# Hash attention and a gated feed-forward block in one kernel: the first unit's gates in groups of three, its value means in the output bank, its first value cast and loads placed elsewhere, and idle products in four slots

## The chip, the cores and the metric

The kernel runs on one core of a Trainium2 chip. A core has five engines that run side by side and wait for one another by semaphores: PE (TensorE, matmuls and transposes, which write to PSUM), DVE (VectorE), ACT (ScalarE), POOL (GpSimd) and SP (SyncE, which here only issues DMAs). ACT and POOL issue DMAs too. Each engine works through its own instructions in the order in which the program gives them. The metric is the device time of one execution in microseconds (us).

## The reference

Two stages, in float32 in and out. The kernel computes matmul operands in 16 bits where the code says so.

```python
q_bits = (np.einsum('bhsd,dk->bhsk', q, proj) > 0)      # 6 bits per token and head
k_bits = (np.einsum('bhsd,dk->bhsk', k, proj) > 0)
mask = q_bucket[:, :, :, None] == k_bucket[:, :, None, :]
scores = np.where(mask, scale * np.matmul(q, k.transpose(0, 1, 3, 2)), -1e9)
attn = softmax(scores)                                   # sum + 1e-9 below the line
x = (attn @ v) as rows of 512                            # 4 batches x 768 tokens = 3072 rows
xn = x / np.sqrt(np.mean(x * x, axis=-1, keepdims=True) + 1e-06) * rms_g
g = xn @ w_gate                                          # 512 -> 1536
out = (g / (1 + np.exp(-g)) * (xn @ w_val)) @ w_out      # 1536 -> 512
```

There are 4 batches, 8 heads of 64, 768 tokens, a model width of 512 and a feed-forward width of 1536.

## The kernel before, in words

**Units and slots.** The 3072 rows are worked through in half batches of 384 tokens, called w = 0 to 7, three blocks of 128 tokens each. The first half batch is split: unit 0 is its first block, unit 1 its other two; units 2 to 8 are whole half batches (`UNITS`, L32). A unit runs over the 8 heads, and each head takes as many slots as the unit has blocks, so unit 0 has slots 0 to 7, unit 1 slots 8 to 23, and later units 24 slots each. A slot is one bank pair of scores (`scores`, L345 to L355, tile s_ps, two buffers) and one exponential over 128x768 on ACT (`probs`, L361, tile psb). The hash mask is part of the score product: 12 rows of signed bits stand under the 64 rows of q and k (tile QK, 76 rows), so that one matmul gives scores with unequal buckets pushed far down.

**The first heads.** For batch 0, `turn_head` transposes k and q of a head on PE (t_ps, L167), copies k to SBUF on DVE and q on ACT (L175), casts k to 16 bits on POOL (`cast_half`, L179) and the first part of q on ACT. `hash_head` (L243) makes the projections on PE (d_ps, L219), DVE turns them into signed bits (`signs`, L226), and the bits go into the QK rows: one or two pieces by a DVE copy (L258), one by ACT, for every second head one more by ACT, the rest by DMA (`late_bits`).

**Products with values.** `av` multiplies the exponentials by the values (o_ps, L375; the output bank has one buffer for a pair of heads). Values are cast to 16 bits on POOL (`v_prep`, L300, tile vl). A column of ones beside the values gives the sum of each row. `v_mean` (L311) sums the values of all tokens of a batch with a matmul by ones into a bank of its own (m_ps, from the three banks of the pool `gps`) and scales them into cvb; `attn_out` adds cvb to the output bank (otmp, L391), takes the reciprocal and multiplies (x, L399: on POOL, for the last pair of heads on DVE). In batch 0 the scaling is done by ACT (L319).

**Norm and feed-forward.** `norm` takes the mean square, the power -1/2 (POOL, L441) and scales rows (xn, L445); `turn_x` transposes them (x_ps, L453) and multiplies by the gain (xnT, L454). `gate` and `value` take one of 12 blocks of the feed-forward width at a time: four matmuls for the gate (g_ps, L470), tanh on ACT (t, L472), four matmuls for the value (v_ps, L481), and two DVE instructions (a, L483; ht, L484). `project` multiplies by the output weights (y_ps, L495), ACT copies the result (ysb, L502) and SP sends it out (L504).

**What sets the order.** The order is written by hand. `plan` holds steps for every slot; `at(s, f, ..., rank=3)` puts a step there, and `steps(s)` sorts a slot's steps by rank and, within a rank, by the order in which they were put down (L583 to L589). In the main loop (L713) a slot s issues the scores of slot s+1 and the exponential of slot s, and then its steps; from slot 24 on, steps of rank below 3 come first, then the exponential of slot s+1, and then the others. `work` (L612) lists for each pair of heads of batches 1 to 3 in which slots its three loads are issued and in which its four transposes are made. `ffn` (L681) spreads the 12 gates and 12 values of a unit over a stretch of slots; a step whose slot is already taken by one of them gets rank 4. Loads go through SP in program order, into ten buffers; SP waits for a buffer's last reader. Weights go through POOL's queue (L543, L549).

Of the kernel before, what the change touches and what calls it, by code (L numbers as in the profile page):

```python
# [16 lines left out]
S = 768  # L17
# [24 lines left out]
def kernel(  # L42
# [188 lines left out]
    def bit_rows(b, h, t):  # L231
        return QK[b, h // 2][D:KROWS, h % 2, t * HALF : (t + 1) * HALF]
# [4 lines left out]
    def bits_tile(i):  # L237
# [3 lines left out]
        return held[-1][:, (i % 2) * HALF : (i % 2 + 1) * HALF]  # L241

    def hash_head(h, n=HALF, k0=None, k1=None):  # L243
        kt, qt = t0(0, h, "k"), t0(0, h, "q")
        ps = hash_bank(
            [(pk[:, 0:32], kt), (pq[:, 0:32], qt), (pk[:, 12:44], kt), (pq[:, 12:44], qt)]
        )
        bt = bits_tile(h)
        signs(bt, ps)
        nc.scalar.copy(bit_rows(0, h, 1)[:, 0:n], bt[32:44, 0:n])  # L250
        for eng, t in ((k0, 0), (k1, 2)):
            src = bt[32 * t : 32 * t + 12]
            if eng is nc.scalar:
                nc.scalar.copy(bit_rows(0, h, t), src)
            elif eng is nc.sync:
                nc.sync.dma_start(out=bit_rows(0, h, t), in_=src)
            else:
                nc.vector.tensor_copy(bit_rows(0, h, t), src)  # L258
        late[h] = bt
# [50 lines left out]
    def v_mean(b, hp, n, parts=(None,)):  # L310
        hs = slice(2 * hp, 2 * hp + n)  # L311
        ps = bank("m_ps", [128, n, 65])
        for i, jt in enumerate(parts):
# [3 lines left out]
            )  # L317
        if b == 0:
            nc.scalar.mul(cvb[b % 2][:, hs, 0:65], ps, C0 / S)  # L319
        else:  # L320
            nc.vector.tensor_scalar_mul(cvb[b % 2][:, hs, 0:65], ps, C0 / S)

# [42 lines left out]
    def av(u, h, i0, i1):  # L365
# [6 lines left out]
        for i in range(i0, i1):  # L372
# [89 lines left out]

    def gate(u, ft):
        w, cs, n = columns(u)
        fs = slice(ft * 128, (ft + 1) * 128)
# [9 lines left out]
    def value(u, ft, gt):  # L475
        g, t = gt
        w, cs, n = columns(u)
        fs = slice(ft * 128, (ft + 1) * 128)
        vv = bank("v_ps", [128, HALF])[:, 0:n]
        for kt in range(4):  # L480
            nc.tensor.matmul(vv, wv[:, kt, fs], xnT[w][:, kt, cs], start=(kt == 0), stop=(kt == 3))  # L481
        a = spool.tile([128, HALF], FP32, name="a")[:, 0:n]
        nc.vector.scalar_tensor_tensor(out=a, in0=t, scalar=1.0, in1=g, op0=ALU.add, op1=ALU.mult)  # L483
        nc.vector.scalar_tensor_tensor(  # L484
            out=ht[w][:, ft, cs], in0=a, scalar=0.5, in1=vv, op0=ALU.mult, op1=ALU.mult
        )
# [3 lines left out]
    def project(w, c, f0, f1):  # L490
# [8 lines left out]
        if f1 == NF:  # L499
# [112 lines left out]
    work = {  # L612
# [50 lines left out]
    for u, (w, c0, n) in enumerate(UNITS):  # L663
        for h in range(H):
            last = BASE[u] + n * h + n - 1
            if n == 1:
                at(last + 1, av, u, h, 0, 6)
                end = last + 1
# [4 lines left out]
            if h % 2:  # L673
                at(end, o_step, u, h // 2)
                if h < 7:
                    if u > 0:
                        at(end + 2 * n, s_step, u, h // 2)
                elif u < 8:
                    at(end, norm, u)

    def ffn(u, s0, ns):  # L681

        seen = set()
        for ft in range(NF):
            for f, s in ((g_step, s0 + (ns * ft) // NF),
                         (v_step, s0 + (2 * ns * ft + ns) // (2 * NF))):
                at(s, f, u, ft, rank=4 if s in seen else 2)
# [100 lines left out]
```

## Time and profile before

| | |
|---|---|
| median of 3 runs | 349.87 us (349.87 to 351.09) |
| profiled execution, its own time | 349.89 us |
| its span, first to last instruction | 348.1 us |
| mean granted TensorE clock | 0.984 |
| PE busy | 334.9 us (96%) |
| DVE busy | 238.2 us (68%) |
| ACT busy | 216.7 us (62%) |
| POOL busy | 138.6 us (40%) |

How to read the profile: the page gives busy times of each engine, the span in 40 equal slices (8.7 us each; a digit is tenths busy; PEclk is the clock that TensorE was granted, in tenths of full speed), and the chain of work that ended last, followed back from the last instruction. A row of a group or of the timeline has the source line, the engine, the operation and the tiles as out<-in, with partitions x elements. A timeline row begins with the start and the duration in us; in [..] stands the idle time of the engine before it and what ended it. The chain's rows have start, duration and what ran. Rows of stretches give, for each stretch, its length and the busy time and number of instructions of PE, PEld (the weight loads, which overlap PE), DVE, ACT and POOL, the granted clock, the share of the DMA engines and GB/s.

### The profile page before, as it was taken

The page shows a single profiled execution, that of the slowest core. Times are in us where ns is not written, and L with a number is a line of the kernel's source. Part 1 is how long each engine was busy: PE and PEld are TensorE (multiplying, and loading weights), DVE is VectorE, ACT ScalarE, POOL GpSimd, SP SyncE. Part 2 cuts the span into 40 slices and gives each one's busy share as a digit, 9 for nine tenths or more (in the row PEclk, how much of TensorE's full clock was granted, in tenths as well). Part 3 has the DMA queues.
Part 4 walks back from the last instruction along what each step waited for, and adds up shares of the span by engine and source line. Part 5 has one row for each costly group of instructions (what it writes and reads, how often), then busy time and mean ns, then how long its engine had stood idle before and what let it go on. Part 6 is the DMA issues. An engine that isn't in the chain of part 4 may idle for free.

```text
span 348.1 us, 8206 instructions
## 1 busy us (share of the span) xinstructions
PE 334.9 (96%) x3172; PEld 212.5 (61%) x3172; DVE 238.2 (68%) x541; ACT 216.7 (62%) x361; POOL 138.6 (40%) x220
## 2 busy tenths in 40 slices
PE   8897998999999999999999999999999999999995
PEld 5456886666666655665566656665566656665553
DVE  3784566688678955897678866897467555675860
ACT  2587687677567755766567756775576766742321
POOL 5476544777214751286126551385111111111000
PEclk9997799999999999999999999999999999999999
DMA  7999944273399005930376008600200010001002
GB/s 216 322 237 190 246 169 89 41 130 80 61 174 149 3 6 145 185 48 5 81 179 119 3 16 200 122 2 6 73 32 1 2 60 33 2 2 74 16 3 90
DMA packets 80199, 31.42 MB, mean 90 GB/s; under 512 B 65240, under 2 KB 77216, under 8 KB 80160
## 3 DMA queue, kind: packets, MB, share of 16 engines
q1 hardware_dynamic: 76176, 26.11, 32.1%
q0 software_dynamic: 3680, 4.72, 7.9%
q8 instruction: 25, 0.41, 0.5%
q14 instruction: 14, 0.11, 0.1%
q10 hardware_dynamic: 304, 0.07, 0.1%
HBM read 28.32 MB, written 6.29 MB: 99 GB/s over the span
## 4 chain that ended last, share of the span: by engine, by line
PE 82%; DVE 11%; issue 3%; ACT 2%; POOL 2%; DVEq 0%; POOLq 0%; ACTq 0%
PE g_ps L470 17%; PE v_ps L481 17%; PE s_ps L351 16%; PE y_ps L495 15%; PE o_ps L375 9%; PE d_ps L219 3%; DVE bits L226 2%; PE x_ps L453 2%; DVE otmp L391 1%; DVE QK L258 1%; DVE xn L445 1%; DVE kT L175 1%; PE y_ps L745 1%; PE m_ps L315 1%; DVE kT L203 1%
## 5 line engine op out<-in xcount | busy, mean ns | idle before, releaser
L361 ACT ACTIVATE psb<-s_ps 128x768 f16<-128x768 f32 x192 | 151.8, 809 | 26.6 <-PE s_ps L351 26.3
L351 PE MATMUL s_ps<-QK 76*128 76x384 f16 (+2 forms) x448 | 96.6, 310 | 0.7 <-ACT psb L361 0.2
L472 ACT ACTIVATE t<-g_ps 128x384 f32<-128x384 f32 (+2 forms) x108 | 49.2, 456 | 55.7 <-PE g_ps L470 54.7
L470 PE MATMUL g_ps<-xnT,wg 128*128 128x384 f16 (+2 forms) x432 | 80.6, 309 | 1.2 <-DVE xnT L454 0.8
L481 PE MATMUL v_ps<-xnT,wv 128*128 128x384 f16 (+2 forms) x432 | 80.6, 309 | 0.7 <-DVE a L483 0.6
L495 PE MATMUL y_ps<-wo,ht 128*128 128x512 f16 x276 | 69.1, 378 | 0.3
L483 DVE SCALAR_TENSOR_TENSOR a<-t,g_ps 128x384 f32<-128x384 f32 (+2 forms) x108 | 53.9, 499 | 21.5 <-ACT t L472 19.8
L375 PEld LDWEIGHTS <-psb 128*128 128x128 f16 x1152 | 52.9, 99 | 19.3 <-issue 5.3
L484 DVE SCALAR_TENSOR_TENSOR ht<-a,v_ps 128x384 f16<-128x384 f32 (+2 forms) x108 | 55.1, 510 | 13.1 <-PE v_ps L481 3.3
L375 PE MATMUL o_ps<-vl,psb 128*128 128x65 f16 x1152 | 58.7, 195 | 2.1 <-DVE otmp L391 1.8
L399 POOL TENSOR_TENSOR x<-otmp,rcp 128x384 f32<-128x384 f32 (+2 forms) x27 | 20.4, 756 | 99.7 <-DVE rcp L396 99.5
L351 PEld LDWEIGHTS <-QK 76*128 76x128 f16 x448 | 40.0, 101 | 25.2 <-issue 1.7
L470 PEld LDWEIGHTS <-wg 128*128 128x128 f16 x432 | 39.2, 97 | 24.1 <-issue 2.9
L481 PEld LDWEIGHTS <-wv 128*128 128x128 f16 x432 | 39.3, 98 | 22.7 <-issue 1.2
L495 PEld LDWEIGHTS <-ht 128*128 128x128 f16 x276 | 24.1, 97 | 20.9 <-issue 0.5
L502 ACT COPY ysb<-y_ps 128x512 f32<-128x512 f32 x23 | 13.5, 586 | 29.4 <-PE y_ps L495 29.1
L391 DVE TENSOR_TENSOR otmp<-o_ps,cvb 128x390 f32<-128x390 f32 (+2 forms) x36 | 18.5, 513 | 17.1 <-PE o_ps L375 14.7
L454 DVE TENSOR_TENSOR xnT<-x_ps,gcol 128x512 f16<-128x512 f16 x24 | 16.6, 691 | 12.7 <-PE x_ps L453 12.6
L211 POOL CAST QK<-kT 64x768 f16<-64x768 f32 x20 | 16.4, 820 | 17.9 <-DVE kT L203 11.6
L226 DVE TENSOR_SCALAR bits<-d_ps,thr,scl 128x384 f16<-128x384 f32 x20 | 13.2, 677 | 12.9 <-PE d_ps L219 12.7
L211 POOL CAST QK<-qT 64x768 f16<-64x768 f32 x20 | 16.4, 820 | 11.9 <-DVE qT L203 11.0
L413 POOL TENSOR_TENSOR sq<-x 128x384 f32<-128x384 f32 (+1 forms) x24 | 19.2, 800 | 1.9
(74 smaller groups left out, 281.6 us busy)
## 6 DMA issues: line engine op xcount, KB each, us to landing
vL<-in_v_dram SPq DMA_DIRECT2D x16, 384.0 KB
out_dram<-ysb SPq DMA_DIRECT2D x23, 256.0 KB
kL<-in_k_dram SPq DMA_DIRECT2D x40, 96.0 KB
qL<-in_q_dram SPq DMA_DIRECT2D x40, 96.0 KB
kL<-in_k_dram SPq DMA_DIRECT2D x5, 384.0 KB
qL<-in_q_dram SPq DMA_DIRECT2D x5, 384.0 KB
wg<-in_moe_w_gate_dram POOLq DMA_DIRECT2D x2, 768.0 KB, 10.6
wv<-in_moe_w_val_dram POOLq DMA_DIRECT2D x2, 768.0 KB, 8.9
```

What stands on the lines that cost most here:

```text
L211: nc.gpsimd.tensor_copy(QK[b, hp][0:64, hh, o : o + S], T0[b, hp, which][64 * hh : 64 * hh + 64, :])
L351: nc.tensor.matmul(ps[:, bk, col : col + ni], k_cols(b, h, jt), q_cols(w, h, 128 * c0 + i0, ni), start=True, stop=True,)
L361: nc.scalar.activation(psb[u, h][:, p], sps.pop(g)[:, :, 0:HALF], AF.Exp, scale=ESCALE,)
L375: nc.tensor.matmul(o[:, c, hh, 0:65], psb[u, h][:, p, bk, col : col + 128], vls[b % 2][:, h, v_chunk(b, h, jt), 0:65], start=(hh == 0 and ...
L391: nc.vector.tensor_add(tmp[:, 0:n, :, 0:65], o[:, 0:n, :, 0:65], cvb[b % 2][:, 2 * hp : 2 * hp + 2, 0:65].unsqueeze(1).to_broadcast([128, ...
L399: eng.tensor_mul(xd.rearrange("p c (h d) -> p c h d", h=2), tmp[:, 0:n, :, 0:64], r[:, 0:n].to_broadcast([128, n, 2, 64]),)
L470: nc.tensor.matmul(g, wg[:, kt, fs], xnT[w][:, kt, cs], start=(kt == 0), stop=(kt == 3))
L472: nc.scalar.activation(t, g, AF.Tanh, scale=0.5)
L481: nc.tensor.matmul(vv, wv[:, kt, fs], xnT[w][:, kt, cs], start=(kt == 0), stop=(kt == 3))
L483: nc.vector.scalar_tensor_tensor(out=a, in0=t, scalar=1.0, in1=g, op0=ALU.add, op1=ALU.mult)
L484: nc.vector.scalar_tensor_tensor(out=ht[w][:, ft, cs], in0=a, scalar=0.5, in1=vv, op0=ALU.mult, op1=ALU.mult)
L495: nc.tensor.matmul(y, ht[w][:, ft, c * 128 : (c + 1) * 128], wo[:, ft, :], start=(ft == 0), stop=(ft == NF - 1),)
```

## The change

- **Bits.** The DVE copies of bits into QK in `hash_head` become `move`: one `scalar_tensor_tensor` that adds zero to the source and takes the maximum with the same source, which leaves the value as it is. There are 13 of them.
- **Value means of batch 0.** `mean0` makes the sums in the output bank of the same pair of heads, in the part that unit 0 leaves unused (its block 1), behind the first of the pair's two products; ACT scales them as before. `v_mean` is used for the later batches alone and stays on DVE there.
- **Value casts.** The first goes ahead of the casts of heads 2 and 3 on POOL; the others are put into slots 1, 3 and 4 at rank 1.
- **Idle products.** `idle(g, n)` makes n products of ones by ones, 128 columns wide, into columns of the next slot's score bank that nothing reads: 6 in slot 4 and 12 in each of slots 5, 6 and 7, 42 in all, as the last step of the slot.
- **Groups.** In unit 0 a step of `gate` or `value` takes three blocks of the feed-forward width at once: 12 matmuls into one bank, one tanh and two DVE instructions over 128x384. The other units keep single blocks.
- **Order.** In unit 0 `av` and `attn_out` get rank 1; in later units `attn_out`, its sum of squares and `norm` get rank 5. The loads of batch 1's first two pairs of heads go three or four slots earlier, their transposes up to five slots earlier, and unit 1's two `turn_x` steps one slot later.
- **First output.** The DMA of the first output block is issued by ACT instead of SP.

```diff
+    def move(dst, src):
+        nc.vector.scalar_tensor_tensor(
+            out=dst, in0=src, scalar=0.0, in1=src, op0=ALU.add, op1=ALU.max
+        )
...
-                nc.vector.tensor_copy(bit_rows(0, h, t), src)
+                move(bit_rows(0, h, t), src)
...
-        if b == 0:
-            nc.scalar.mul(cvb[b % 2][:, hs, 0:65], ps, C0 / S)
-        else:
-            nc.vector.tensor_scalar_mul(cvb[b % 2][:, hs, 0:65], ps, C0 / S)
+        nc.vector.tensor_scalar_mul(cvb[b % 2][:, hs, 0:65], ps, C0 / S)
...
+    def mean0(hp):
+        for c in range(6):
+            nc.tensor.matmul(
+                ot[0, hp][:, 1, :, 0:65], ones16, vls[0][:, 2 * hp : 2 * hp + 2, c, 0:65],
+                start=False, stop=(c == 5), skip_group_check=True,
+            )
+        nc.scalar.mul(cvb[0][:, 2 * hp : 2 * hp + 2, 0:65], ot[0, hp][:, 1, :, 0:65], C0 / S)
+
+    def idle(g, n):
+        for _ in range(n):
+            nc.tensor.matmul(
+                sps[g][:, 1, HALF:], ones16, ones16, start=True, stop=True,
+                skip_group_check=True,
+            )
...
+    GROUP = [3] + 8 * [1]
...
-        g = bank("g_ps", [128, HALF])[:, 0:n]
-        for kt in range(4):
-            nc.tensor.matmul(g, wg[:, kt, fs], xnT[w][:, kt, cs], start=(kt == 0), stop=(kt == 3))
-        t = spool.tile([128, HALF], FP32, name="t")[:, 0:n]
+        g = bank("g_ps")[:, 0 : k * n]
+        for j in range(k):
+            fs = slice((f0 + j) * 128, (f0 + j + 1) * 128)
+            for kt in range(4):
+                nc.tensor.matmul(
+                    g[:, j * n : (j + 1) * n], wg[:, kt, fs], xnT[w][:, kt, cs],
+                    start=(kt == 0), stop=(kt == 3),
+                )
+        t = spool.tile([128, HALF], FP32, name="t")[:, 0 : k * n]
...
-            nc.sync.dma_start(out=rows[:, out_chunk(w, c), :], in_=ysb)
+            eng = nc.scalar if (w, c) == (0, 0) else nc.sync
+            eng.dma_start(out=rows[:, out_chunk(w, c), :], in_=ysb)
...
+    v_prep(0, 0)
     turn_head(2, 128)
...
-    for hp, s in enumerate((0, 1, 3, 4)):
-        at(s, v_prep, 0, hp)
+    for hp, s in ((1, 1), (2, 3), (3, 4)):
+        at(s, v_prep, 0, hp, rank=1)
...
-        at(2 * hp + 2 if hp < 3 else 7, v_mean, 0, hp, 2, range(6))
+        at(2 * hp + 1, mean0, hp, rank=2)
...
-        (1, 0): ((21, 22, 23), (28, 29, 30, 31)), (1, 1): ((24, 25, 26), (33, 34, 35, 36)),
+        (1, 0): ((18, 19, 22), (24, 25, 26, 27)), (1, 1): ((20, 21, 23), (28, 29, 32, 33)),
...
-                at(last + 1, av, u, h, 0, 6)
+                at(last + 1, av, u, h, 0, 6, rank=1)
...
-                at(end, o_step, u, h // 2)
+                at(end, o_step, u, h // 2, rank=1 if u == 0 else 5)
...
-                        at(end + 2 * n, s_step, u, h // 2)
+                        at(end + 2 * n, s_step, u, h // 2, rank=5)
...
-                    at(end, norm, u)
+                    at(end, norm, u, rank=5)
...
+        k = GROUP[u]
+        m = NF // k
+        for i in range(m):
+            for f, s in ((g_step, s0 + (ns * i) // m), (v_step, s0 + (2 * ns * i + ns) // (2 * m))):
+                at(s, f, u, k * i, rank=4 if s in seen else 2)
...
+    for s, n in ((4, 6), (5, 12), (6, 12), (7, 12)):
+        at(s, idle, s + 1, n, rank=6)
...
-    at(29, turn_x, 1, 1, rank=1)
-    at(30, turn_x, 1, 2, rank=1)
+    at(30, turn_x, 1, 1, rank=1)
+    at(31, turn_x, 1, 2, rank=1)
```

More of the change, by code (lines that the diff above doesn't have):

```diff
@@ L461, in columns, with gate, value @@
         return w, slice(128 * c0, 128 * (c0 + n)), 128 * n
[L463 removed]
+    GROUP = [3] + 8 * [1]
+    def gate(u, f0):
         w, cs, n = columns(u)
[L465 removed]
+        k = GROUP[u]
         if w not in ht:
             ht[w] = hpool.tile([128, NF, HALF], FP16, name="ht")
[L468 to L471 removed]
+        g = bank("g_ps")[:, 0 : k * n]
[7 more added lines that the diff above has]
+        t = spool.tile([128, HALF], FP32, name="t")[:, 0 : k * n]
         nc.scalar.activation(t, g, AF.Tanh, scale=0.5)
         return g, t
[L475 removed]
+    def value(u, f0, gt):
         g, t = gt
         w, cs, n = columns(u)
[L478 to L482, printed above, removed]
+        k = GROUP[u]
+        vv = bank("v_ps")[:, 0 : k * n]
+        for j in range(k):
+            fs = slice((f0 + j) * 128, (f0 + j + 1) * 128)
+            for kt in range(4):
+                nc.tensor.matmul(
+                    vv[:, j * n : (j + 1) * n], wv[:, kt, fs], xnT[w][:, kt, cs],
+                    start=(kt == 0), stop=(kt == 3),
+                )
+        a = spool.tile([128, HALF], FP32, name="a")[:, 0 : k * n]
         nc.vector.scalar_tensor_tensor(out=a, in0=t, scalar=1.0, in1=g, op0=ALU.add, op1=ALU.mult)
         nc.vector.scalar_tensor_tensor(
[L485 removed]
+            out=ht[w][:, f0 : f0 + k, cs], in0=a.rearrange("p (k n) -> p k n", k=k), scalar=0.5,
+            in1=vv.rearrange("p (k n) -> p k n", k=k), op0=ALU.mult, op1=ALU.mult,
         )
```

7 lines of the change are left out of this document (1 added, 6 removed).

## The prediction

> **What bounds the kernel now.** I read the page first (busy shares, slices with the granted clock, the chain of waits), then the chain, the timelines and the stretches of the first 62 us, the only part in which the change reorders PE by more than a few instructions.
>
> The page, slices and shares of the chain:
>
> ```profile
> PE   8897998999999999999999999999999999999995
> PEclk9997799999999999999999999999999999999999
> PE 82%; DVE 11%; issue 3%; ACT 2%; POOL 2%; DVEq 0%; POOLq 0%; ACTq 0%
> ```
>
> PE bounds the kernel from about 40 us on: a PE instruction saved there is time saved, and work on ACT or DVE is not. The two 7s of PEclk, about 26 to 44 us, are the one place with a lower granted clock, and they lie in the stage that the change edits. The chain just ahead of them:
>
> ```profile
> 26.17 0.69 DVE bits L226
> ...
> 27.18 0.51 ACT QK L254
> 27.69 0.02 issue
> 27.72 0.29 ACT cvb L319
> 28.03 0.30 DVE otmp L391
> 28.33 0.05 issue
> 28.38 0.36 PE o_ps L375 x6
> ```
>
> The sign test of the last head ends at 26.85 (I call this moment T); after it ACT moves bits, makes the value mean cvb, DVE reads the output bank, and only then PE goes on, 1.77 us after its last matmul. Stretches of 3.41 us, laid so that one begins where the clock falls (columns: us, then busy us and counts of PE, PEld, DVE, ACT, POOL, granted clock, DMA share, GB/s):
>
> ```profile
> 22.92:26.33 3.41, 3.19 (x44) 1.68 (x45) 3.13 (x7) 2.43 (x6) 2.50 (x5) 1.00 1.22 210
> 26.33:29.74 3.41, 1.63 (x29) 1.35 (x30) 1.83 (x4) 2.60 (x6) 2.41 (x4) 1.00 1.15 177
> 29.74:33.16 3.42, 3.42 (x34) 2.95 (x31) 1.14 (x5) 2.80 (x6) 2.01 (x5) 0.50 1.16 201
> 36.57:39.98 3.41, 3.41 (x36) 3.17 (x34) 1.32 (x5) 1.26 (x3) 0.96 (x3) 0.50 1.18 245
> 39.98:43.40 3.42, 3.32 (x64) 3.10 (x62) 2.25 (x9) 2.69 (x6) 2.23 (x5) 1.00 1.15 276
> 53.64:57.05 3.41, 2.49 (x23) 1.40 (x21) 2.16 (x10) 3.17 (x5) 0.90 (x2) 1.00 0.22 78
> ```
>
> PE was busy 48% of the stretch before the fall; the clock then stayed at 0.50 for 10.24 us. The stretch at 53.64, 73% busy, was followed by no fall. Slots 14 and 24 on ACT:
>
> ```profile
> 39.09 0.80 ACT L361 ACTIVATE psb<-s_ps 128x768 f16<-128x768 f32 x1
> ...
> 49.86 1.56 ACT L361 ACTIVATE psb<-s_ps 128x768 f16<-128x768 f32 x2
> ```
>
> Slot 14 starts at T+12.24, slot 24 at T+23.01. Last, the copies of bits that the change replaces, and the rows nearest to what replaces them:
>
> ```profile
> L258 DVE COPY QK<-bits x13: 250/498/872, 9.2 to 26.9; 12x384 f16<-12x384 f16 x13
> ```
> ```profile
> L408 DVE SCALAR_TENSOR_TENSOR sq<-x x23: 285/286/292, 54.7 to 314.2; 128x128 f32<-128x128 f32 x23
> ```
> ```profile
> 203.78 0.45 POOL L308 TENSOR_TENSOR vsum<-vadd 128x128 f16<-128x128 f32 x1
> ...
> 203.94 0.70 DVE L399 TENSOR_TENSOR x<-otmp,rcp 128x384 f32<-128x384 f32 x1
> ```
>
> **The change part by part.** The sum is made against the profiled execution: 348.1 us of span, 349.89 in all, 0.02 over the median.
>
> *Before T (DVE-bound: 4.72 of the 5 us from 15 to 20).* A copy takes 0.25 with POOL idle; where a POOL cast was running it ended 0.115 after that cast (the 0.85 to 0.87 us copies stand beside 0.82 us value casts). The new instruction is of L408's kind, one tensor read twice: 286 ns for 128 elements, 693 for 512 (L429), so 0.557 for 384, and 1.04 for two in a row (L408's start 0.22 apart). It lies between two ends. Never held: the pair behind the second sign test costs +0.52 (1.04 against 11.89 to 12.41, POOL idle); the eight behind the sign tests of heads 2 to 6 take 4.24 instead of 0.82+0.48+1.45+0.50+1.42=4.67, so -0.43. Held by every cast: L399 reads two SBUF tensors and took 703 instead of its median 557 beside a POOL add; it ended 0.41 after that add, so each held one ends 0.3 later than the copy did: up to seven, +2.1. Two other pieces: the first value mean is now made on ACT two steps earlier, which takes away DVE's 0.66 wait for cvb before 23.06; the second otmp and reciprocal (0.33) now stand in front of T. Never held that makes 0.52-0.43-0.66+0.33=-0.24, held by all +1.9. I take one or two held, **+0.2**: the first value cast moves into POOL's idle 9.6 to 13.0 and others swap places, so the collisions of before need not recur; but one row is thin evidence, so both ends stay. The value cast waits for its load ahead of head 2's and 3's casts; the load is the seventh on its queue, 1.97 MB through it, and 2.36 MB had moved by 10 us (159 and 312 GB/s in two stretches of 5), so by estimate it has landed. Two new waits of ACT for a mean stand in front of its query copies; PE makes them at once behind products that ACT has released, so I cost them at nothing, covered by DVE, the bound here. POOL's weight DMA issues move behind that value cast or swap with head 5's casts by under 1 us; the weights they bring land at 20.9 to 45.5 and are first used after 37, so they cost nothing while landings stay ahead of use.
>
> [...]
>
> *T to slot 14.* Slot 5's exponential follows two ACT copies (0.29+0.51): T+0.85, where before it stood behind cvb too (27.89). The idle products are written into the bank that the next exponential reads and stand behind that slot's products and mean on PE, so exponentials 5 to 8 wait for them. Twelve take 0.66 at the gates' rate (four 128-wide in 0.22) or 1.37 at that of the 27 warm-up products (3.09 us); I take 0.66, the same form at full clock. PE in slots 5 to 7: scores 0.33, products 0.18, mean 0.36 in every other, idle 0.66; exponential 8 comes at T+4.5 (before 31.19, T+4.34). With the output bank no longer waiting on the last step of ACT, and 42 products in the gap, PE is idle at most about 1.1 of any 3.41 us here: 68% busy, between 48% (fell) and 73% (did not), nearer the latter. I take a full clock. Then 0.75 per slot (three in 2.28 at 54.89): slot 13 at T+8.3. The first gates wait for otmp, norm and xnT: 32.41 to 37.08 before, 4.67, less 0.21 for the half-clock transpose; otmp now at T+5.0, gates T+9.45, three blocks 0.66, tanh of 384 from 0.15 later (491 ns, 0.4 to the next): slot 14 at T+10.55. **-1.7.** If the clock falls again, about 0.
>
> [...]
>
> *Slots 14 to 24.* PE's sum is unchanged: 10 slots of 0.51, seven groups of 0.66, 9.7 us, where 10.77 passed. ACT drops from 0.28 a block to 0.4 a group. But a group comes in one piece: tanh waits for all twelve gate products, and the next exponential stands behind tanh. Slot by slot (scores may start when the exponential two before has ended) the four gate slots cost 1.6 with tanh, the value slots 1.17 and the others 0.75, partly overlapped: 10.5. **-0.3**, between -1.1 (PE's sum) and +0.8 (no overlap). DVE's 24 instructions of 0.29 become 8 of 0.5, hidden: DVE was busy 7.32 of these 10.77.
>
> *Slots 24 to 60.* Transposes of batch 1 come three to five slots earlier, loads three or four; SP issued these at 33.9 to 37.0, far ahead. xnT now stands behind one more sign test (0.69) on DVE, and the transposes that filled PE's 0.78 wait at 57.04 are partly gone: +0.2. PE's waits of 0.32, 0.21, 0.23 and 0.39 between 64 and 83 should shrink with the earlier transposes: -0.4. The first output's DMA goes to ACT's queue (0.57 between ACT's two issues at the start; ACT waits for PE there), SP loses an 18 us wait (36.97 to 55.02) that held up transfers that are not late. Later otmp (rank 5): PE waits for it once in the kernel, 1.8 us, so nothing from 75 us on. **-0.2**, from -0.9 to +0.9.
>
> Sum: +0.2-1.7-0.3-0.2=-2.0, and 349.89-2.0=**347.9**.
>
> **Rivals.**
> (a) The clock falls all the same in slots 4 to 9. For: 68% is below anything seen to survive. Against: 48% is far below. The 1.7 is lost: 349.6.
> (b) Slower: the clock falls later, where exponentials bound slots 9 to 13 and PE does only 0.51 in 0.75 (68%) and then waits for xnT. It decides if one 3.41 us stretch there drops under the unknown bound between 48% and 73%. Then the gates' 9.7 us of PE work meet 10.24 us at half speed: about 5 more, 353.
> (c) Every move is held: +1.7 over the sum, 349.6. For: the L399 row. This is also the case in which replacing the copies does the opposite of relieving DVE.
> (d) Groups overlap as PE's sum allows (-0.8) and the stalls of 57 to 83 go altogether (-1.0): 346.1.
>
> **How the numbers follow.** Forecast with its own range 346.5 to 349.2: 0.55; (a) 0.15, (b) 0.08, (c) 0.12, (d) 0.10. Half a per cent, about what a measurement of this kernel can tell, is 1.75 us, so faster means below 348.1. The forecast's 0.55 puts 0.40 below that, 0.13 within, 0.02 beyond; (d) is faster; (a) and (c) are mostly within, 0.05 of them slower; (b) slower: 0.51 faster, 0.34 same, 0.15 slower. The range 345.9 to 351.0 takes in all but (b) and the tails.
>
> **What would show it.** Right: no 0.50 in the granted clock between 26 and 45 us; otmp of the second pair ahead of the last sign test; T between 26.6 and 27.8; slot 14 about 10.5 after T, slot 24 about 10.5 after that; from 90 us on the same distances as before. Wrong: a fall of the clock anywhere ahead of 50 us; new DVE moves of 0.7 or more beside casts (then T at 28 or later); ACT waits for idle products of over 0.5 per slot; PE waiting over 1.5 for xnT at about 57.

## The result, and the profile after

The changed kernel takes 354.62 us (median of 4 runs, 353.84 to 355.16) where the kernel before takes 350.21 beside it: a ratio of 1.012, 95% interval 1.009 to 1.015. It is slower; the forecast was 347.9, with 351.0 as the upper end of its range. The profiled execution took 355.16, with a span of 353.4, 5.3 us more than the one before.

The page of the changed kernel, slices and shares of the chain:

```profile
PE   8887898997999999999999999999999999999995
PEclk9999999999899999999999999999999999999999
PE 79%; DVE 11%; ACT 3%; issue 3%; POOL 2%; DMA 1%; SPq 1%; DVEq 0%; ACTq 0%; POOLq 0%
```

The two 7s of PEclk at 26 to 44 us are gone, as forecast. An 8 has come at 88 to 97 us, and two names are new in the chain: DMA and SP's queue. That stage lay outside the part I had studied. Around the last sign test, the chain of waits:

```profile
25.74 0.75 DVE QK L245
26.49 0.03 issue
26.52 0.30 DVE otmp L409
...
27.02 0.58 DVE bits L226
...
27.93 0.52 ACT QK L260
28.45 0.02 issue
28.46 0.82 ACT psb L362
...
29.82 0.18 PE o_ps L376 x6
30.00 0.67 PE s_ps L396 x12
```

The sign test ends at 27.59 (T, 0.74 later than before), the second otmp stands in front of it, and PE goes on with idle products where it had been idle. Twelve take 0.67, as reckoned. Stretches of 3.41 us (columns as in the prediction):

```profile
26.50:29.91 3.41, 2.38 (x47) 2.23 (x45) 1.58 (x4) 2.29 (x6) 1.89 (x3) 1.00 1.07 147
33.33:36.74 3.41, 2.61 (x34) 1.95 (x33) 1.80 (x6) 3.40 (x5) 2.20 (x7) 1.00 1.07 335
84.53:87.94 3.41, 1.22 (x11) 0.73 (x10) 1.65 (x4) 1.23 (x2) 0.01 (x1) 1.00 1.01 216
87.94:91.35 3.41, 3.41 (x20) 0.89 (x18) 1.28 (x3) 0.81 (x1) 2.46 (x3) 0.50 0.32 49
```

The first two kept a full clock at 70% and 77% busy. The third, 36% busy, was followed by the one at 0.50. Slots 14 and 24 on ACT (slot 24 is the third exponential of its row, 49.28):

```profile
38.17 0.49 ACT L497 ACTIVATE t<-g_ps 128x384 f32<-128x384 f32 x1 [1.44 <-PE g_ps L492]
38.56 1.51 ACT L362 ACTIVATE psb<-s_ps 128x768 f16<-128x768 f32 x2
...
47.83 2.27 ACT L362 ACTIVATE psb<-s_ps 128x768 f16<-128x768 f32 x3
```

Step by step, changed minus before, from the starts of the exponentials (T is the end of the last sign test):

| step | forecast | measured | from |
|---|---|---|---|
| before T | +0.2 | +0.74 | 27.59 against 26.85 |
| T to slot 14 | -1.7 | -1.27 | 10.97 against 12.24 |
| slots 14 to 24 | -0.3 | -0.05 | 10.72 against 10.77 |
| slots 24 to 60 | -0.2 | +4.98 | 58.10 against 53.12 |
| slot 60 to the end | 0 | +0.87 | the rest of 5.27 |

So up to slot 24 the change gained 0.58, and then it lost 5.85. Most of that falls in one place, slots 49 to 51 (+0.43 to +4.40). The chain there:

```profile
80.06 0.34 PE s_ps L352 x2
80.40 0.32 SPq L118
80.76 1.45 SPq L118
82.25 0.65 SPq L118
82.94 3.12 DMA qL<-in_q_dram
86.19 0.85 DVE qT L203
87.04 0.26 DVE a L513
87.35 1.32 PE y_ps L526 x4
```

The last part of a load of q is issued by 82.94 and lands at 86.06; a DVE transpose waits for it, the feed-forward's instruction a stands behind that transpose, and PE waits 2.19 us for a; it then works at half clock for 3.41 us, busy throughout, which by estimate costs another 1.7 (half of 3.41). Why the load was late stands in SP's queue, first of the changed kernel, then of the kernel before (start, length of the issues, tile):

```profile
60.10 6.20 SPq L280 DMA_DIRECT2D QK<-bits  x8
66.40 3.37 SPq L118 DMA_DIRECT2D qL<-in_q_dram  x4
...
73.75 6.20 SPq L280 DMA_DIRECT2D QK<-bits  x8
80.06 3.53 SPq L118 DMA_DIRECT2D qL<-in_q_dram  x4
```

```profile
58.32 2.65 SPq L118 DMA_DIRECT2D qL<-in_q_dram  x4
63.33 6.20 SPq L276 DMA_DIRECT2D QK<-bits  x8
...
74.28 2.89 SPq L118 DMA_DIRECT2D qL<-in_q_dram  x4
77.27 6.18 SPq L276 DMA_DIRECT2D QK<-bits  x8
```

The eight small DMAs that bring a pair's bits into QK follow that pair's transposes. With the transposes moved up they are issued ahead of the next pairs' loads of q, and each set holds SP for 6.2 us. Before, each q load stood ahead of the bits; the last one was issued 5.8 us earlier.

### The profile page after: what moved, and what is told of

Read it like the earlier page. It is cut to its first block, busy times and chain, and to the rows that moved or that the text cites. A ratio compares the mean times of both kernels' runs of the same rounds, so it can differ in the third digit from the quotient of the medians.

```text
span 353.4 us, 8264 instructions
## 1 busy us (share of the span) xinstructions
PE 335.6 (95%) x3214; PEld 211.6 (60%) x3214; DVE 239.1 (68%) x525; ACT 215.1 (61%) x353; POOL 140.5 (40%) x220
## 3 DMA queue, kind: packets, MB, share of 16 engines
q0 software_dynamic: 3680, 4.72, 7.8%
## 4 chain that ended last, share of the span: by engine, by line
PE 79%; DVE 11%; ACT 3%; issue 3%; POOL 2%; DMA 1%; SPq 1%; DVEq 0%; ACTq 0%; POOLq 0%
PE g_ps L492 16%; PE v_ps L508 16%; PE y_ps L526 15%; PE s_ps L352 14%; PE o_ps L376 8%; PE d_ps L219 4%; PE x_ps L471 1%; DVE a L513 1%; DVE qT L203 1%; PE t_ps L167 1%; DVE bits L226 1%; DVE otmp L409 1%; DVE xn L463 1%; ACT psb L362 1%; DMA qL<-in_q_dram 1%
## 5 line engine op out<-in xcount | busy, mean ns | idle before, releaser
L352 PE MATMUL s_ps<-QK 76*128 76x384 f16 (+2 forms) x448 | 94.7, 303 | 3.8 <-ACT psb L362 3.7
L497 ACT ACTIVATE t<-g_ps 128x384 f32<-128x384 f32 (+1 forms) x100 | 47.8, 478 | 55.8 <-PE g_ps L492 54.6
L492 PE MATMUL g_ps<-xnT,wg 128*128 128x384 f16 (+2 forms) x432 | 78.8, 307 | 2.2 <-DVE xnT L472 1.9
L508 PE MATMUL v_ps<-xnT,wv 128*128 128x384 f16 (+2 forms) x432 | 78.8, 307 | 0.9 <-DVE a L513 0.7
L513 DVE SCALAR_TENSOR_TENSOR a<-t,g_ps 128x384 f32<-128x384 f32 (+1 forms) x100 | 53.1, 531 | 31.7 <-ACT t L497 30.3
L514 DVE SCALAR_TENSOR_TENSOR ht<-a,v_ps 128x384 f16<-128x384 f32 (+1 forms) x100 | 53.8, 538 | 13.1 <-PE v_ps L508 2.8
L376 PEld LDWEIGHTS <-psb 128*128 128x128 f16 x1152 | 51.4, 97 | 16.9 <-issue 5.0
L376 PE MATMUL o_ps<-vl,psb 128*128 128x65 f16 x1152 | 57.7, 193 | 0.7 <-DVE otmp L409 0.7
L352 PEld LDWEIGHTS <-QK 76*128 76x128 f16 x448 | 38.7, 98 | 29.4 <-issue 4.3
```

What stands on the lines that cost most here:

```text
L352: nc.tensor.matmul(ps[:, bk, col : col + ni], k_cols(b, h, jt), q_cols(w, h, 128 * c0 + i0, ni), start=True, stop=True,)
L376: nc.tensor.matmul(o[:, c, hh, 0:65], psb[u, h][:, p, bk, col : col + 128], vls[b % 2][:, h, v_chunk(b, h, jt), 0:65], start=(hh == 0 and ...
L492: nc.tensor.matmul(g[:, j * n : (j + 1) * n], wg[:, kt, fs], xnT[w][:, kt, cs], start=(kt == 0), stop=(kt == 3),)
L508: nc.tensor.matmul(vv[:, j * n : (j + 1) * n], wv[:, kt, fs], xnT[w][:, kt, cs], start=(kt == 0), stop=(kt == 3),)
L514: nc.vector.scalar_tensor_tensor(out=ht[w][:, f0 : f0 + k, cs], in0=a.rearrange("p (k n) -> p k n", k=k), scalar=0.5, in1=vv.rearrange("p ...
```

## The experiments

All times are compared with the kernel before on the same chip. The starts of the exponentials in the profiled executions, less those of the kernel before, in us, tell the stages apart (slot 13: before the first gates; 57: behind the late load; 191: the last):

```
kernel                          slot 4     13     14     24     25     43     57    191
changed kernel                  +0.69  +0.22  -0.53  -0.58  -0.00  +0.41  +4.39  +5.25
1 batch-1 order as before       +0.68  +0.36  +0.29  +0.24  +0.82  +0.83  +0.82  +1.67
2 two loads ahead of the bits   +0.56  +0.08  -0.67  -0.72  -0.15  +0.27  +0.27  +1.11
3 no idle products              +0.70  +0.74  +0.42  +1.11  +1.68  +2.10  +2.74  +3.58
4 idle products alone           +0.09  +0.59  -0.18  -0.59  -0.59  -0.58  -0.56  -0.57
5 = 2, ranks 3                  +0.72  +0.26  -0.49  -0.54  +0.03  +0.45  +0.47  +0.48
6 = 2, copies                   -0.80  -1.63  -1.63  -1.32  -0.75  -0.31  -0.31  +0.55
7 = 2, single blocks            +0.70  +0.23  -0.55  -0.18  +0.59  +1.01  +1.02  +1.86
8 means, cast, idle products    +0.72  +0.04  -0.73  -1.14  -1.13  -1.15  -1.16  -1.16
9 = 8, moves                    +0.70  +0.23  +0.38  +0.05  +0.05  +0.04  +0.04  +0.04
10 = 8, groups, values rank 4   -0.34  -1.35  -2.09  -2.07  -2.12  -2.20  -2.22  -2.22
11 = 8, no idle products        -0.33  -2.10  -2.12  -2.52  -2.52  -2.52  -2.52  -2.22
12 = 4, of 32 rows              +0.01  +4.74  +4.44  +4.03  +4.03  +4.02  +4.03  +4.03
```

A row of this table is one execution. Whether the clock falls for one stretch between slots 9 and 14 can differ from execution to execution of the same kernel (by the granted clock, five of ten executions of number 1 and five of ten of number 2 lost one stretch; the profiles of numbers 1, 6, 9 and 11 have such a fall; before, 3 and 12 fell earlier and for longer), and a stretch of 3.41 us at 0.50 takes 0.005 off the granted clock of the whole execution (0.995 in the changed kernel's profile, which has one). Where it matters, times are therefore given at equal granted clock as well.

**1 and 2. The order of batch 1, and the loads alone.** Number 1 takes back the slots of batch 1's loads and transposes; number 2 keeps them and moves only two loads of q ahead of the bits.

```diff
-        (1, 0): ((18, 19, 22), (24, 25, 26, 27)), (1, 1): ((20, 21, 23), (28, 29, 32, 33)),
+        (1, 0): ((21, 22, 23), (28, 29, 30, 31)), (1, 1): ((24, 25, 26), (33, 34, 35, 36)),
...
-    at(30, turn_x, 1, 1, rank=1)
-    at(31, turn_x, 1, 2, rank=1)
+    at(29, turn_x, 1, 1, rank=1)
+    at(30, turn_x, 1, 2, rank=1)
```

> The changed kernel with the places of batch 1's first two pairs of heads (loads, transposes) and of the second unit's two transposes of x put back as before; all else stays changed. Theory A (in the changed kernel SP issues the bits of these pairs ahead of the query loads of the next pairs, and the late load of the last pair holds DVE and then PE at slot 50): the 4.0 us that slots 49 to 51 lost go, and the time is 350.0 to 350.8. Rival B (the loss comes from the groups, moves and idle products ahead of slot 24, and slot 50 only shows it): 354 to 355.

```diff
-        (1, 2): ((27, 30, 33), (35, 37, 39, 40)), (1, 3): ((32, 35, 39), (41, 43, 45, 47)),
+        (1, 2): ((27, 27, 33), (35, 37, 39, 40)), (1, 3): ((32, 33, 39), (41, 43, 45, 47)),
```

> The changed kernel with two entries altered: the query load of batch 1's third pair goes from slot 30 to 27 and that of the fourth pair from 35 to 33, so that SP issues both ahead of the bits of the pair before; transposes and everything else stay where the change put them. Theory A (order on SP's queue): slot 50 comes within 0.6 of its time in the kernel before and the time is 350.2 to 351.0. Rival C (it is the earlier transposes themselves, on DVE and PE, that cost): 353.5 or more.

Measured: 351.18 us, ratio 1.005 (1.002 to 1.008), and 351.61, ratio 1.006 (1.003 to 1.008), both medians above what theory A said. Five of ten executions of each lost one stretch (granted clock 0.994 or 0.995) and took 351.6 to 351.9 and 352.0 to 352.3; the other five took 350.7 to 350.8 and 350.7 to 351.2. The 4 us at slots 49 to 51 are gone in both. Number 2 changes nothing but the place of two loads in SP's queue, so it was that queue and not the earlier transposes as such; number 1 leaves the first output's DMA on ACT's queue, so it was not that either. In its rows the q load now stands ahead of the second set of bits:

```profile
70.89 2.76 SPq L118 DMA_DIRECT2D qL<-in_q_dram  x4
73.75 6.18 SPq L280 DMA_DIRECT2D QK<-bits  x8
```

The changed order of batch 1 costs 0.4 even so: from slot 25 to 43 number 2 loses 0.42, number 1 0.01. No run tells here between the transposes, their loads and the later `turn_x`. Number 1 also shows a thing that the changed kernel escaped: its clock fell at 35.40 for 3.41 us, on the way from slot 13 to 14, although its instructions up to there are the same. It is taken up at number 12.

**3 and 4. The idle products, out of the changed kernel and alone in the kernel before.**

```diff
-    for s, n in ((4, 6), (5, 12), (6, 12), (7, 12)):
-        at(s, idle, s + 1, n, rank=6)
```

> The changed kernel without its 42 idle products. Theory (they keep the clock): a stretch at 0.50 comes back ahead of 45 us, and slot 24 is 1.2 to 2 us later than with them. Rival (closing the wait for the output bank is enough): the clock stays at 1.00, and the exponentials of slots 7 and 8, which wait 0.62 and 0.45 for idle products, come up to 1 us earlier. The total may hide either, since the late load at slot 50 absorbs up to about 0.5; slot 24 decides.

> The kernel before with the 42 idle products alone added in slots 4 to 7. Theory (more PE work near the 1.77 us gap keeps the clock full): no stretch at 0.50, slot 14 about 1.5 earlier, 348.4 to 349.4. Rival (the gap is a wait for the last step of ACT, stays, and the clock falls all the same): the products' 2.3 us delay slots 5 to 8 by 0.5 to 1, 350.4 to 351.2.

Measured: 353.37 us without them, ratio 1.009 (1.006 to 1.011); 349.50 with them alone, ratio 0.999 (0.996 to 1.002).

Without them the clock falls at 30.46 for 10.24 us, as in the kernel before, and slot 24 comes 1.7 us later than in the changed kernel. Alone in the kernel before they keep the clock full and bring slot 24 forward by only 0.59, since exponentials 6 to 8 wait up to 1.5 us for them first; slot 14 came 0.18 earlier, not 1.5.

The price of that wait shows in the kernel before, which now and then keeps its clock by itself: three of its executions beside these runs were granted 0.998 and took 347.5 us (most of the others had 0.984 to 0.990 and took 349.6 to 349.9), where the seven of number 4 at 1.00 took 348.7 to 349.8. So the idle products do keep the clock, worth about 2.3 us here, but cost about 1.7 of it themselves.

(Number 3's median lies below the changed kernel's although slot 24 is later: the late q load landed at 86.0 in both, so work that arrived 1.7 us later waited 0.49 for it instead of 2.19, and the clock did not fall behind that shorter wait.)

**5. Ranks.** Number 2, with rank 3 again for attn_out, its sum of squares and norm in the later units.

```diff
-                at(end, o_step, u, h // 2, rank=1 if u == 0 else 5)
+                at(end, o_step, u, h // 2, rank=1 if u == 0 else 3)
...
-                        at(end + 2 * n, s_step, u, h // 2, rank=5)
+                        at(end + 2 * n, s_step, u, h // 2)
...
-                    at(end, norm, u, rank=5)
+                    at(end, norm, u)
```

> The kernel with both query loads ahead of the bits, and besides rank 5 taken back to 3 for the output step, the sum of squares and the norm of the later units; only DVE's order differs from the kernel with the loads ahead. Theory (rank 5 lets every half batch lose 0.04 to 0.2 from slot 72 on): the last exponential, +1.11 against the kernel before, comes to +0.3, and the time is 0.8 below that with the loads ahead, 350.5 to 351. Rival (the drift comes from elsewhere, as the prediction had it, where rank 5 costs nothing): +1.1 stays.

Measured: 350.28 us, ratio 1.004 (1.002 to 1.005). The loss of 0.83 between slots 57 and 191 is gone. With rank 5 most of it came in three jumps of 0.21 at slots 97, 121 and 145, the second slots of units 5, 6 and 7: otmp and the reciprocal stood on DVE ahead of the a and ht of the unit before, and PE's next value block began 0.37 us after the start of the last score product instead of 0.16.

The 0.57 between slots 24 and 25 stayed. It is PE's wait for the output bank in the changed kernel, with DVE's rows ahead of it:

```profile
47.96 0.55 DVE L513 SCALAR_TENSOR_TENSOR a<-t,g_ps 128x384 f32<-128x384 f32 x1 [1.76 <-ACT t L497]
48.63 0.55 DVE L514 SCALAR_TENSOR_TENSOR ht<-a,v_ps 128x384 f16<-128x384 f32 x1
49.10 0.41 DVE L436 TENSOR_REDUCE ssp<-sq 128x2 f32<-128x256 f32 x1
49.43 0.42 DVE L409 TENSOR_TENSOR otmp<-o_ps,cvb 128x260 f32<-128x260 f32 x1
```

```profile
49.90 0.34 PE L376 MATMUL o_ps<-vl,psb 128*128 128x65 f16 x6 [0.71 <-DVE otmp L409]
```

otmp of unit 1 lies behind the last a and ht. In the kernel before it ran at 49.00, ahead of the last block's. A value group has its slot to itself and so rank 2, ahead of otmp at rank 3 as well as at rank 5.

**6 and 7. Copies for the moves, single blocks for the groups**, each in number 2.

```diff
-                move(bit_rows(0, h, t), src)
+                nc.vector.tensor_copy(bit_rows(0, h, t), src)
```

> The kernel with both query loads ahead of the bits, and the 13 moves made DVE copies again. Theory (moves held behind POOL's casts and longer than a copy): slots 1 to 4 come 0.5 to 0.9 earlier, the end of the last sign test 0.6 to 0.9 earlier, and slot 24 too. Rival (never held, as long as the copies): no slot moves by more than 0.25.

```diff
-    GROUP = [3] + 8 * [1]
+    GROUP = 9 * [1]
```

> The kernel with both query loads ahead of the bits, and the first unit's gates and values one block at a time again. Theory (a group in one piece makes the next exponential wait for twelve products and a tanh, and saves only ACT time): slot 14 comes 0.3 to 0.8 earlier, slot 25 by 0.6 to 1.2. Rival (ACT bounds these slots, so fewer tanh pay): slot 25 comes 0.3 or more later.

Measured: 350.45 us, ratio 1.003 (1.001 to 1.004), with copies; 352.20, ratio 1.009 (1.006 to 1.011), with single blocks. The copies bring slot 4 forward by 1.36 and slot 13 by 1.7 (T at 25.74), so the moves had cost far more than T's 0.74; mean and early cast had paid for a part of it. In the two profiles 0.6 of that 1.7 is left at the end, but that of number 6 lost the clock at 34.44 for 3.41 us and that of number 2 kept it. At equal granted clock most of the gain stays (on two chips, on both of which the kernel before took 347.5 where it kept its clock): 349.6 to 349.7 against 350.7 to 351.2 at 0.998 or more, 350.4 to 350.6 against 352.0 to 352.3 at 0.994 or 0.995.

With single blocks slot 14 did not come earlier (+0.12) and slot 25 came 0.74 later, so the theory failed and the rival had the number. But not its reason: set beside number 8, also of single blocks, number 7 loses 0.78 at slot 21 and 0.77 at slot 25, and PE waits 0.9 us for otmp, which rank 5 puts behind one more a and ht. Slots 14 to 24 take 10.37 us with single blocks at rank 3 (numbers 4 and 8), 10.73 with groups at either rank (the changed kernel, numbers 2 and 5) and 11.14 with single blocks at rank 5.

The moves' rows in the changed kernel, and POOL's casts beside one of them:

```profile
11.89 1.11 DVE L245 SCALAR_TENSOR_TENSOR QK<-bits 12x384 f16<-12x384 f16 x2
...
17.94 0.79 DVE L245 SCALAR_TENSOR_TENSOR QK<-bits 12x384 f16<-12x384 f16 x1
...
23.05 0.55 DVE L245 SCALAR_TENSOR_TENSOR QK<-bits 12x384 f16<-12x384 f16 x1
24.98 1.51 DVE L245 SCALAR_TENSOR_TENSOR QK<-bits 12x384 f16<-12x384 f16 x2
```

```profile
17.26 1.06 POOL L179 CAST QK<-kT 64x384 f16<-64x384 f32 x2 [0.36 <-DVE kT L175]
18.39 1.03 POOL L304 CAST vl<-vL 128x768 f16<-128x768 f32 x1
...
26.89 0.82 POOL L304 CAST vl<-vL 128x768 f16<-128x768 f32 x1
```

A move took 0.55 with POOL idle (both of the row at 11.89). The one at 17.94 began while the casts of 17.26 ran, which ended at 18.32; it took 0.79 and ended 0.41 behind them, and the value cast that began beside it at 18.39 took 1.03 instead of 0.82. So in these rows each held the other, and the one that began second ended late: the move at 15.28, which began ahead of a 64x384 cast at 15.34, took 0.55, and that cast 0.86 instead of 0.50. Five of the thirteen moves were lengthened this way, and each ended 0.41 us behind the cast, as in the row of L399 that the prediction went by. The rows of the thirteen moves make 8.35 us, those of the thirteen copies in number 8 4.75.

**8. A kernel of the parts that had gained**: the changed kernel with copies, single blocks, ranks 3, batch 1's order and the first output's queue as before. What remains is value means in the output bank, unit 0's ranks, the first cast early, and the idle products.

> The changed kernel with copies for moves, single blocks, ranks of later units, the order of batch 1 and the first output's queue as before: what is left of the change is the value means in the output bank with the first unit's ranks, the value casts' places and the idle products. Theory (the gain lies in these, every other part costs): full clock, slot 25 0.9 to 1.5 ahead of the kernel before, no loss later, 348.3 to 349.0. Rival (the means bring nothing, the idle products alone did it): the same -0.56 as with idle products alone, 349.2 to 349.5.

Measured: 347.32 us, ratio 0.9955 (0.9937 to 0.9974), the lowest median here. It is faster than both kernels, than the one before by under half a per cent. All seven executions were granted a clock of 1.00. Against number 4 it gains 2.2 us; which of means, ranks and cast brings that, no run tells. Its profiled execution took 348.73, since q's transposes for head 6 waited 0.88 us at 20.95 (probably for their load; T at 27.41 instead of 26.02 in number 10); six other runs took 347.2 to 347.9.

**9 to 11. Number 8 with one thing changed**: moves for the copies; groups of three, with their values at rank 4; no idle products.

```diff
-                at(s, f, u, k * i, rank=4 if s in seen else 2)
+                at(s, f, u, k * i, rank=4 if s in seen or (k > 1 and f is v_step) else 2)
```

> The kernel of the run before it that took 347.32 us, with the thirteen DVE moves of the change in place of its copies, and nothing else. Theory M (what the moves cost before the last sign test stays in the total): swapping moves for copies in the kernel with the loads ahead took 1.7 us off slot 13 and 0.59 off slot 50, so this kernel should be 0.6 to 1.7 us above 347.3, thus 347.9 to 349.0, with slot 13 about 1 us later than with copies and every later slot by the same. Rival N (the moves hide behind waits for loads and do not matter for the total): in the profiled execution with copies slots 4 to 8 started within 0.2 us of those with moves, so this kernel should be within 0.3 of 347.3.

> The kernel that took 347.32 us, with gates and values of the first unit in groups of three again, the value groups at rank 4, so that otmp of unit 1 stays ahead of the last group's two DVE instructions. Theory G (grouping itself gains, and what it lost was DVE's order behind it): in the pair with and without groups slot 24 came 0.54 us earlier with them, and PE then waited 0.71 us for otmp; with otmp ahead that wait goes, so slots 24 and 25 both start about 0.5 us earlier than with single blocks and the median is near 346.8. Rival H (grouping only moves the wait): slot 25 starts where it did, and the median stays within 0.2 of 347.3.

> The kernel that took 347.32 us without the 42 idle products. Theory K (they keep the clock full between slots 4 and 13): one stretch ahead of 45 us is granted 0.50, slot 24 starts 1.2 to 1.9 us later (1.7 in the pair of the changed kernel with and without them), and the median is 348.5 to 349.2. Rival L (with value means in the output bank and copies, PE's gap at slots 5 to 7 is short enough without them): the clock stays full, slots 5 to 8 start about 1 us earlier, and the median is 346.5 to 347.3.

Measured: 349.05 us, ratio 0.999 (0.998 to 1.001); 347.72, ratio 0.996 (0.994 to 0.998); 348.44, ratio 0.998 (0.995 to 1.000). The moves cost 1.7 by the medians, 1.3 by the ratios: theory M, toward the upper end; T is 27.60, and the clock falls at 36.24 for 3.41 us.

With the groups and otmp in front, PE's 0.71 wait is gone (slots 24 to 25 lose nothing), so G named the wait rightly, but the median is 0.4 above number 8's, beyond the 0.2 of rival H too. Slots 14 to 25 take 11.50 us with the groups and 11.12 without: the groups cost what is missing.

Without idle products the clock of the profiled execution falls at 33.01 for 3.41 us, as theory K has it, but slot 24 does not come later. Slots 5 to 13 no longer wait for idle products and reach slot 13 0.75 earlier than in number 10, which also had its loads early; the fall takes that back by slot 14. One profile misleads here: five of twelve executions without idle products were granted 0.984 or 0.985, as much as the kernel before loses, and took 348.7 to 349.9, while one at 0.998 took 346.56, less than any with them. By the medians they are worth 1.1 us (347.32 against 348.44, just under K's 348.5), by the ratios to the kernel before 0.7, with intervals that overlap; the time is also steadier, 347.24 to 348.73 with them.

**12. Filled columns and the clock.** The full clock records of the kernel before last 23.89, 10.24 and 307.20 us, those of the changed kernel 81.92, 3.41 and 262.83: 7, 3, 90, 24, 1 and 77 times 3.413. If stretches of 3.41 us are laid on the beat of each execution's clock records, busy time does not sort them. Number 4's lowest stretch was 49% busy and kept the clock; numbers 1 and 9 lost it behind 73% and 67%. Counting for each matmul the columns it moves, times the rows that it fills over 128, the most in any row of the profiles, over 8192 columns, sorts all of them (at 0.50 the kernel before starts its 128-column gate products 0.107 us apart, which makes about 4096 columns in 3.41 us, and 8192 is twice that): in the thirteen profiled executions so far, every stretch between 18 and 90 us with at most 0.371 filled was followed by 0.50, every one with 0.375 or more by a full clock, from either state. (Counting float32 once, twice or four times moves no stretch across the bound.) Some of these stretches, among them the nearest to the bound on either side:

```
profiled execution    stretch from   PE busy   filled columns   clock after
changed kernel        84.53          0.36      0.28             0.50
before                26.34          0.48      0.28             0.50
number 9              32.83          0.67      0.28             0.50
number 11             29.60          0.74      0.33             0.50
number 1              31.99          0.73      0.36             0.50
before (at 0.50)      29.75          1.00      0.371            0.50
number 4              33.57          0.76      0.375            1.00
changed kernel        33.33          0.77      0.385            1.00
number 4              26.75          0.49      0.40             1.00
before (at 0.50)      36.58          1.00      0.43             1.00
```

A value product has 128 rows, a score product 76 (`128*128` and `76*128` in the rows of PE); slots 9 to 13 lie close to the bound (0.36, 0.375 and 0.385 above), so by estimate a shift of the stretches' beat against the program decides there: numbers 1 and 2, whose instructions there are the changed kernel's, each lost one stretch in five executions of ten. The test was number 4 with idle products of 32 rows: the same columns and busy time, a quarter of the fill.

```diff
-                sps[g][:, 1, HALF:], ones16, ones16, start=True, stop=True,
+                sps[g][:, 1, HALF:], ones16[0:32], ones16[0:32], start=True, stop=True,
```

> The kernel before with the 42 idle products alone, each of 32 rows instead of 128: the same number of products, the same 128 columns each, thus the same busy time of PE, but a quarter of the rows of the array. With 128 rows the clock stayed full although the lowest stretch of 3.41 us (from 26.75) was only 49% busy, as little as the one ahead of the fall in the kernel before (48%). Theory R (what counts is columns moved times rows filled): over twelve profiles each stretch with at most 0.371 of what a full array could take was followed by half clock and each with 0.375 or more by full clock; the twelve idle products of that stretch carry 0.19 of its 0.40, so with 32 rows it drops to about 0.26 and the clock falls to 0.50 ahead of 31 us, for 3.4 to 10.2 us, with slot 24 some 0.5 to 2 us later than with 128 rows. Rival S (what counts is PE's busy time, or columns alone, and the stretch before had some other flaw): busy time and columns are unchanged, the clock stays full as with 128 rows, and slot 24 starts at 49.3.

Measured: 353.79 us, ratio 1.011 (1.008 to 1.015). The clock fell at 29.24 for 13.65 us, four stretches (columns as before), first number 12, then number 4:

```profile
25.83:29.24 3.41, 1.89 (x34) 1.51 (x31) 2.31 (x5) 1.81 (x5) 2.41 (x5) 1.00 1.08 159
29.24:32.65 3.41, 3.41 (x35) 2.98 (x32) 0.46 (x2) 1.09 (x2) 1.15 (x3) 0.50 1.12 196
32.65:36.07 3.42, 3.42 (x32) 2.89 (x31) 0.00 (x0) 1.17 (x3) 1.37 (x3) 0.50 1.13 182
36.07:39.48 3.41, 3.15 (x27) 2.38 (x26) 1.45 (x5) 2.95 (x4) 0.55 (x2) 0.50 1.14 266
39.48:42.89 3.41, 3.41 (x38) 2.91 (x36) 1.45 (x3) 1.90 (x3) 2.75 (x7) 0.50 1.16 269
```

```profile
26.75:30.16 3.41, 1.69 (x35) 1.69 (x36) 1.50 (x4) 2.35 (x5) 2.19 (x4) 1.00 1.18 190
```

Theory R holds in kind, though the fall was longer than the 3.4 to 10.2 us that it set, and slot 24 came 4.6 later than with 128 rows, not 0.5 to 2: at half clock the idle products themselves, of 128 columns like the gates above, take by estimate twice as long (0.107 us each; the changed kernel's start 0.055 to 0.056 apart at full clock). PE was busier than in number 4 (1.89 against 1.69) and lost the clock, and in the two stretches behind the fall it was busy without a gap and still did not get it back. By the count these hold 0.18, 0.26, 0.26, 0.28 and 0.40, and only behind the last did the clock return.

All eight executions were granted 0.985 or less, all ten of number 4 0.995 or more. The bound's size was fitted to these runs; the test shows that here the same products with a quarter of the rows lost the clock. Whether the columns of the array that a product fills count too, these stretches can't tell: counting them changes none of these numbers.

## Why the prediction was wrong, step by step

**The step that failed is "Slots 24 to 60".** It named SP's queue and judged it by the wrong DMAs: "SP issued these at 33.9 to 37.0, far ahead" is true of the loads that move, and "SP loses an 18 us wait ... that held up transfers that are not late" counts only what gets easier. A transpose brings its pair's eight bit DMAs with it, and these were never listed; they passed two q loads and cost 4.1 us (number 2 against the changed kernel). The same step gave the earlier transposes -0.4 and xnT +0.2; the new order of batch 1 came out at +0.4 in all. It had no term for otmp behind the value group, +0.57, which groups and rank 5 each bring about.

**Its last term, "so nothing from 75 us on",** failed by 0.83 (numbers 2 and 5). I had asked where PE waits for otmp; the price was what otmp, moved back, does to the a and ht that now follow it.

**Before T**: the mechanism was right and its size off. The term was "one or two held"; five moves in four of the six rows behind heads 2 to 7 were held (a pair 1.33 to 1.51, a single 0.79), and a pair unheld took 1.11, not 1.04. Against the copies the moves cost 1.6 us of T (27.6 in number 9, 26.0 in number 10).

**T to slot 14**: the clock stayed full and slots 8 and 13 came at T+4.72 and T+8.34, close to 4.5 and 8.3. That the clock held behind slot 9 was luck in part: with the same instructions up to there, numbers 1 and 2 lost one stretch in half of their executions, and number 1's profile shows it there. Gates began at T+9.71 instead of 9.45 and tanh later still: 0.4 of the 1.7 was missing, 0.1 of it in the sum itself (9.45, 0.66, 0.15 and 0.4 make 10.66, not 10.55).

**Slots 14 to 24** gained 0.05 instead of 0.3, and not by the groups. The 10.77 us of before began with 0.89 at half clock; at full clock the same single blocks take 10.37 (numbers 4 and 8), so the full clock gave 0.41 and the groups cost 0.36. They overlap little: tanh waits 0.6 to 1.4 us for its twelve products each time. (Without overlap the prices listed make 11.7 for the three gate, four value and three other slots, so that end was +1.0, not +0.8.)

Of the rivals, (a) did not come. The mechanism of (b), a fall behind slots 9 to 13, came in numbers 1, 6, 9 and 11, for one stretch of 3.41 us and about 1 us, not 5; in the changed kernel the profiled execution escaped it. (c) came in part. The bound "between 48% and 73%" that I took for (a) and (b) was not borne out: 49% busy was kept (number 4), 74% was not (number 11). No rival asked what SP's queue puts ahead of a later load.

## What to carry to other kernels

When a step moves, list every DMA that it issues and each queue's later entries that these pass; a row of small DMAs (here 6.2 us for eight) ahead of one load can cost more than all the rest of the edit. Price a move by the instructions that now stand behind it on its engine, not only by who waits for the step itself. Filler products kept the clock here with 128 rows and lost it with 32, and they delayed what read behind them (exponentials 6 to 8 by up to 1.5 us): in the kernel before, the two nearly cancelled (ratio 0.999, 0.996 to 1.002), in number 8 they were worth about 1 us by the medians. Where the clock depends on the execution (0.984 to 1.00 among the twelve of number 11), one profile is not enough; look at the granted clock of every execution before a difference is put down to an edit.

## What the runs showed of the hardware

In these traces the granted clock followed columns times filled rows in stretches of 3.41 us, not PE's busy time: in number 12 the clock stayed at 0.50 behind a stretch 100% busy at 0.26 filled, in number 4 at 1.00 behind one 49% busy at 0.40. In the changed kernel a DVE move, which reads one tensor twice, took 0.55 us with POOL idle and 0.730 to 0.795 behind a POOL cast that had begun first, ending 0.41 us after that cast; a value cast took 1.03 us beside a move that was held and 0.82 without one. On SP the issues of a pair's eight bit DMAs took 6.18 to 6.20 us between 60 and 84 us, 0.78 for one, about as long as one of the four parts of a q load (2.65 to 3.53 for four).
